# A planner that knows when each tile is written, read and loaded

## The chip, the cores and the metric

The kernel runs on one core of a Trainium2 chip. The core has five engines that take their instructions each from a list of its own, strictly in order: TensorE (PE in the profile; PEld is its weight load), VectorE (DVE), ScalarE (ACT), GpSimd (POOL) and SyncE (SP). An instruction whose operand is not there yet holds up everything behind it on its engine, and nothing on the others. Transfers between main memory and the on-chip memory are issued here by SP and by POOL, each with a queue of its own.

The metric is device time in microseconds (us) of one execution; the figure for a kernel is the median over several runs.

## The reference

The output mixes two branches, row by row, with a gate `g`. The first branch is linear attention with 32 heads of 20, the second a gated linear unit. The sequence has 2048 rows, the model width is 640, the hidden width 1536, all in fp32:

```python
phi = lambda t: where(t > 0, t + 1, exp(t)) + 1e-6
q, k, v = split(x @ wqkv)                     # 640 -> 3 x 640, 32 heads of 20
kv  = einsum("bhsd,bhse->bhde", phi(k), v)
z   = phi(k).sum(rows)
a   = (phi(q) @ kv) / (phi(q) . z + 1e-6) @ wo
b   = (sigmoid(x @ w_gate) * (x @ w_up)) @ w_down
g   = sigmoid((x * gate_w).sum(-1))
out = g * a + (1 - g) * b
```

## The kernel before

*Products.* Each fp32 operand is split into a high part, which ScalarE rounds (`split`, `act`), and a low part, which VectorE gets by subtraction. A product is then three matmuls, high by high, high by low and low by high (`mm3`, lines 216 to 218, so every matmul of the trace has one of these three lines). In the same way nearly all work of ScalarE is on line 227 and nearly all of VectorE's on line 231: the tile names tell the steps apart. Large products are cut into 2 x 2 blocks and computed with seven products of sums of blocks where eight would be the plain way. The sums are VectorE's work, the splits of the sums ScalarE's and VectorE's.

*Stages*, with their place on the trace of before: the K stage (to 142 us) makes phi(k), its sums and the products of phi(k) with x (tiles `pk`, `xn`, `gt`). Then come two passes over pairs of token groups of 512 columns, pass 1 first. Each has a q phase (`q_phase`: 142 to 191 and 414 to about 460), which makes phi(q), and in pass 1 also the attention's matrix (`kv_part`, `m_part`; tiles `wo_sb`, `woh`, `ms`), and an f phase (`f_phase`: 191 to 402, and 448 to 660), which goes over 12 chunks of the hidden width. `last_down` closes a pass; the A phase at the end (668 to 734) applies the attention's matrix and adds both branches.

*The f phase.* For each chunk f a `Block` has steps s1 to s7 (tiles `ch`, `dd`, `cc` in the accumulators; `c11`, `c12`, `c22`, `cx` in memory). Beside each odd f from 3 on runs `down_pair`, which multiplies the hidden tiles of two earlier chunks (`hf`) by the down weights (`wd`, `ds`, or `wf` in pass 0) in the products W, X0, V, X1, Y1, Y0, Z0, Z1 and adds their results to `tb`. In it `new` starts an accumulator, `go` adds a product, `out` lets ScalarE or VectorE read it into `tb`. A matmul that adds to an accumulator after an `out` has to wait until the `out` has read it. Each q or f weight comes as a `wst` tile (`load_w`) and is turned into the tiles `wg`, `wu`, `ws` by `queue_g` and `queue_s` in pass 1, stored in main memory, and loaded again in pass 0 (`load_form`). Down weights come as `dst` (`load_d`) and become `wd` and `ds`. The denominators of the attention (`queue_dens`) are a chain in pass 0: `pden` tiles are loaded, VectorE sums them into `fac`, the result goes out to memory and comes back reordered. `queue_m` splits the attention's matrix (`mr` loaded, `mt` split and stored) in pass 0 as well.

*The order.* The schedule is manual: each engine's list is the order in which the program issues. TensorE's order is written out by the phases. Everything for ScalarE and VectorE that need not follow a product at once is put in a queue of the planner `Order` (line 30): `add` takes a function with its cost on ScalarE (`a`) and VectorE (`v`), a key, and `ready`, the earliest time. While the program is written the planner keeps three modelled clocks, `pe`, `act` and `vec`. After each step `fill` takes the next item from `urgent`, `items`, `lazy`, `chain` and `spare`, in this order, if `_fits` says that it ends within a slack (0.6 and 1.2 us, or 1.6 and 2.4) of `pe`. Before a product that reads a tile `need(key)` issues what is still queued for it. Loads are believed to be there a fixed time after their issue, such as

```python
st["at", g, u] = max(order.pe, order.vec) + 9.0    # queue_dens, a pden tile
```

and a product is believed to be ready when TensorE's clock has come to it, whatever its operands. These clocks decide only the order; on the chip, semaphores make each instruction wait for its data.

Of the kernel before, what the change touches and what calls it, by code (L numbers as in the profile page):

```python
# [14 lines left out]
P = 128  # L15
# [14 lines left out]
class Order:  # L30

    def __init__(self):
        self.slack(False)
        self.pe = self.act = self.vec = 0.0
        self.items, self.lazy, self.chain, self.spare, self.soon, self.urgent = [], [], [], [], [], []
        self.kept = []
        self.busy = False
        self.parts = self.pend = None
# [5 lines left out]
    def add(self, a, v, fn, key=None, ready=None, lazy=False, first=False, chain=False, spare=False,  # L44
            kept=False):
# [27 lines left out]

    def _run(self, it):
# [12 lines left out]
    def _fits(self, it):  # L87
        a, v, fn, key, ready = it
        if ready is not None and self.pe < ready():
            return False  # L90
# [4 lines left out]
    def fill(self):  # L95
        if self.busy:
            return
        while True:
# [4 lines left out]
            for q, n in ((self.urgent, len(self.urgent)), (self.items, 1), (self.lazy, 1), (self.chain, 1), (self.spare, 1)):  # L103
# [4 lines left out]
            else:  # L108
# [5 lines left out]
                return  # L114

# [22 lines left out]
    def need(self, key, now=True):  # L138
        self.follow_up(max((i + 1 for i, f in enumerate(self.soon) if f[3] == key), default=0))
        while (it := next((it for it in self.urgent if it[3] == key), None)) is not None:  # L140
# [3 lines left out]
            if now:  # L144
                self.pe = max(self.pe, self.act, self.vec)
        for q in (self.items, self.lazy, self.chain, self.spare, self.kept):
# [3 lines left out]
            if last >= 0 or self.pend and self.pend[1] == key:  # L150
                self._flush()
                if now:
                    self.pe = max(self.pe, self.act, self.vec)
# [15 lines left out]
    def on_act(self, w, after):  # L169
        t = self._after(after)  # L170
        self.act = max(self.act, t) + a_cost(w)

    def on_vec(self, w, after, rate=1.0):
        t = self._after(after)
        self.vec = max(self.vec, t) + v_cost(w * rate)

# [9 lines left out]
def gated_mix_kernel(ctx: ExitStack, tc: tile.TileContext, xt, xn, wk, wv, wo, wst_q, wst_f, out_t):  # L186
# [6 lines left out]
    order = Order()  # L193

# [20 lines left out]
    def mm3(out, l_hi, l_lo, r_hi, r_lo, first, last):  # L215
# [3 lines left out]
        order.on_pe(3, width(out))  # L219
# [5 lines left out]
    def act(out, src, fn, after="", **kw):  # L225
        order.on_act(width(out), after)
        nc.scalar.activation(out, src, fn, **kw)  # L227

    def vec2(out, a, b, op, after=""):
        order.on_vec(width(out), after)  # L230
        nc.vector.tensor_tensor(out, a, b, op=op)  # L231

    def vec3(out, a, scalar, b, op0, op1, after=""):
        order.on_vec(width(out), after)
        nc.vector.scalar_tensor_tensor(out, a, scalar, b, op0=op0, op1=op1)

    def vec1(out, a, s0, s1=None, op0=OP.mult, op1=None, after=""):
        order.on_vec(width(out), after)
# [104 lines left out]
    class Chunk:  # L343
# [7 lines left out]
        def load(self, parts=((0, 0, KC), (1, 0, KC)), lag=0.0):  # L351
            for b, k0, k1 in parts:
                nc.sync.dma_start(self.x[b][:, k0:k1],
# [112 lines left out]
    for k in range(KC):  # L466
        nc.sync.dma_start(xst[:, 0, k], xt[0, :, k, :CW])
        if k:
            nc.sync.dma_start(wk_st[k], wk[k * P:(k + 1) * P])
        else:  # L470
            nc.sync.dma_start(wk_st[0][:, HW:], wk[:P, HW:])
        nc.sync.dma_start(xst[:, 1, k], xt[1, :, k, :CW])
# [56 lines left out]
    def queue_qw(u):  # L529

        raw = qs.tile([P, 2, D], F32, name="qraw", tag="qraw")
        nc.sync.dma_start(raw, wst_q[:, u:u + 2])
# [3 lines left out]
        def piece(i, c, src):  # L536
            n = width(src)

            def fn():
                t = qs.tile([P, 2, w], F32R, name="qp", tag="qp", bufs=2)  # L540
                split(t[:, 0, :n], t[:, 1, :n], src)
                order.then(lambda: nc.sync.dma_start(w_dram["q", u, i][:, :, c:c + n], f32(t[:, :, :n])))
# [32 lines left out]
    def load_xn(n):  # L575
        if n < 16:
            i = tok(n // 2, n % 2)
            t = m1_tile("mb", "xnst")
            nc.sync.dma_start(t, xn[i * P:(i + 1) * P])
# [24 lines left out]
    def vec_copy(out, src, after=""):  # L604
        order.on_vec(width(out), after)
# [114 lines left out]
    def z_add(r):  # L720

        nc.gpsimd.dma_start(zacc.rearrange(view2, j=2), r, accum_op=OP.add if z_started else OP.bypass)
# [115 lines left out]
    for c in range(1, 4):  # L838
# [76 lines left out]
        if c == 3:  # L915
# [23 lines left out]
            def store_w(n, i):  # L939
# [3 lines left out]
                nc.gpsimd.dma_start(w_dram[key], f32(WT[n, i]))  # L943
# [8 lines left out]
            nc.sync.dma_start(f32(WT[("q", 1, 2), 0]), w_dram["q", 2, 0])  # L952
# [17 lines left out]
        else:  # L970
            w_stage = m1_tile("ma", "w0")
            nc.sync.dma_start(w_stage, wst_q[:, KC - 1])
# [47 lines left out]
    def load_form(n, i):  # L1020
        t = (wg_tile, wu_tile, ws_tile)[i]()
        nc.sync.dma_start(f32(t), w_dram[n[::2] + (i,)])
# [7 lines left out]
    def load_w():  # L1030
        t = pw2.tile([P, 2, D], F32, name="wst", tag="wst", bufs=2)
        if not w_loads:
            t = t.rearrange("p k c -> p (k c)").rearrange("p (k c) -> p k c", c=CW)
            nc.sync.dma_start(t, xt[len(c1_x), :, :, CW:])
            c1_x.append(t)
            other[-1].at = order.pe + 4.0
            return
        n = w_loads.pop(0)
        nc.sync.dma_start(t, wst_f[n[2], :, 0:2] if n[0] == "f" else wst_q[:, 0:2])
        WST[n] = t  # L1040
        W_AT[n] = order.pe + (8.0 if n[0] == "f" else 4.0)

    def queue_q(u):
# [6 lines left out]
        order.add(a_cost(D), v_cost(D), fn, ("wg", m), lambda: DST[m][1], first=True)  # L1050

    def queue_g(n):

        order.add(a_cost(D), v_cost(D), lambda: wg_split(n, WST[n][:, 0]), ("wg", n), lambda: W_AT.get(n, 1e9),
                  first=n[2] != 1)

    def queue_s(n, first=0, last=2):

        def sums(part):
            g, u = WST[n][:, 0], WST[n][:, 1]  # L1060
            c = [slice(2 * i * P, 2 * (i + 1) * P) for i in range(2)]
            if part == 0:
                order.need(("wg", n), False)
                add(u[:, c[1]], u[:, c[0]], u[:, c[1]])
# [1315 lines left out]
```

## Time and profile before

| | |
|---|---|
| median of 3 runs | 738.40 us (738.03 to 738.62) |
| profiled execution | 739.57 us |
| its span | 737.6 us |
| TensorE busy | 729.6 us, 99% |
| VectorE busy | 563.7 us, 76% |
| ScalarE busy | 354.5 us, 48% |
| GpSimd busy | 95.2 us, 13% |
| granted TensorE clock | 1.00 |

The profile is one execution. The time of an execution is longer than the span, which goes from the first instruction to the end of the last. "Busy" counts the time in which an engine has an instruction in work; matmuls overlap each other, so that TensorE can be counted as busy while it waits a short time. In a row of the timeline stand the start, the length, the engine, the line, the operation, the tile written and the tiles read, the shape, and in brackets the idle time before it and what ended that. "x2" means two such instructions in one row.

### The profile page before, as it was taken

The numbers are of one execution on the slowest core, as the hardware profiler recorded it, in microseconds if no ns is written. First come the engines' busy times: TensorE is split into PE (matmuls) and PEld (weight loads), VectorE is DVE, ScalarE is ACT, GpSimd is POOL, SyncE is SP. The second block draws the span as 40 slices with busy tenths as digits, with TensorE's granted clock in tenths as the row PEclk, the third lists the DMA queues.
The fourth block names the chain that finished last, engine by engine and source line by source line (L and its number), as shares of the span: only waits on it lengthen the run. The fifth ranks groups of instructions, "written<-read, shape, count | busy, mean of one in ns | idle before, by whom it ended". The sixth has DMA issues, their size and how long they took to land.

```text
span 737.6 us, 10091 instructions
## 1 busy us (share of the span) xinstructions
PE 729.6 (99%) x3575; PEld 621.3 (84%) x3575; DVE 563.7 (76%) x987; ACT 354.5 (48%) x661; POOL 95.2 (13%) x161
## 2 busy tenths in 40 slices
PE   9999999999999999999999999999999999999998
PEld 8999999987777888888888888888888788888886
DVE  4988778987687889898988942447686767689993
ACT  5764638366555654535363364354423232423550
POOL 0210111123221202020200211000000032000000
PEclk9999999999999999999999999999999999999999
DMA  7573658697969766666875457967969797859212
GB/s 254 140 206 94 186 127 256 155 323 282 313 222 349 258 240 239 238 229 243 303 286 208 176 179 281 330 198 263 352 205 310 264 366 196 315 197 347 109 72 101
DMA packets 71001, 173.54 MB, mean 235 GB/s; under 512 B 11642, under 2 KB 32394, under 8 KB 67238
## 3 DMA queue, kind: packets, MB, share of 16 engines
q1 hardware_dynamic: 54582, 109.99, 45.6%
q0 software_dynamic: 16224, 62.74, 24.0%
q8 instruction: 28, 0.46, 0.3%
q14 instruction: 23, 0.19, 0.1%
q10 hardware_dynamic: 144, 0.16, 0.1%
HBM read 103.96 MB, written 63.92 MB: 228 GB/s over the span
## 4 chain that ended last, share of the span: by engine, by line
PE 89%; issue 3%; DMA 3%; ACT 2%; DVE 1%; POOL 1%; POOLq 0%; ACTq 0%
PE ch L218 9%; PE ch L216 9%; PE ch L217 9%; PE cc L216 8%; PE cc L218 7%; PE cc L217 7%; PE dd L216 7%; PE dd L217 7%; PE dd L218 7%; PE rot L216 6%; PE rot L217 6%; PE rot L218 6%; DMA wo_sb<-wo 1%; DMA wd<-ds 1%; ACT c L227 0%
## 5 line engine op out<-in xcount | busy, mean ns | idle before, releaser
L227 ACT ACTIVATE c<-ch 128x512 f32<-128x512 f32 x52 | 31.0, 597 | 95.9 <-PE ch L218 95.9
L231 DVE TENSOR_TENSOR hf<-c,hf 128x512 fp32r<-128x512 f32 x75 | 51.0, 687 | 27.9 <-ACT hf L227 27.8
L227 ACT ACTIVATE hf<-c 128x512 fp32r<-128x512 f32 x75 | 46.1, 624 | 41.0 <-DVE c L231 40.9
L231 DVE TENSOR_TENSOR c<-cc,c 128x512 f32<-128x512 f32 x40 | 27.5, 689 | 37.2 <-PE cc L218 21.2
L216 PE MATMUL ch<-xth,ws 128*128 128x512 f32 x112 | 44.2, 394 | 1.1 <-ACT c L227 0.5
L218 PE MATMUL ch<-xth,ws 128*128 128x512 f32 x112 | 43.7, 391 | 0.1
L217 PE MATMUL ch<-xtl,ws 128*128 128x512 f32 x112 | 43.6, 389 | 0.0
L231 DVE TENSOR_TENSOR tb<-rot,tb 128x512 f32<-128x512 f32 (+1 forms) x59 | 37.9, 674 | 4.7 <-PE rot L218 4.1
L231 DVE TENSOR_TENSOR tb<-dd,tb 128x512 f32<-128x512 f32 x44 | 30.1, 685 | 10.5 <-PE dd L218 10.5
L216 PE MATMUL dd<-xrh,wg 128*128 128x512 f32 x90 | 35.1, 390 | 0.0
L218 PE MATMUL dd<-xrh,wg 128*128 128x512 f32 x90 | 35.0, 389 | 0.0
L217 PE MATMUL dd<-xrl,wg 128*128 128x512 f32 x90 | 35.0, 389 | 0.0
L231 DVE TENSOR_TENSOR c<-c,c 128x512 f32<-128x512 f32 x46 | 31.6, 686 | 2.6 <-ACT c L227 2.0
L216 PE MATMUL cc<-xbh,ws 128*128 128x512 f32 x84 | 32.7, 389 | 0.0
L217 PE MATMUL cc<-xbl,ws 128*128 128x512 f32 x84 | 32.7, 389 | 0.0
L218 PE MATMUL cc<-xbh,ws 128*128 128x512 f32 x84 | 32.7, 389 | 0.0
L231 DVE TENSOR_TENSOR wst<-wst 128x256 f32<-128x256 f32 (+2 forms) x69 | 27.4, 412 | 1.4
L216 PE MATMUL rot<-pkh,xnh 128*128 128x320 f32 x90 | 28.0, 311 | 0.0
L217 PE MATMUL rot<-pkl,xnh 128*128 128x320 f32 x90 | 27.8, 309 | 0.0
L218 PE MATMUL rot<-pkh,xnl 128*128 128x320 f32 x90 | 27.8, 309 | 0.0
L227 ACT ACTIVATE c<-dd 128x512 f32<-128x512 f32 x22 | 13.0, 592 | 29.3 <-PE dd L218 26.2
L216 PEld LDWEIGHTS ch<-xth,ws 128*128 128x128 f32 x112 | 21.0, 188 | 6.8 <-ACT c L227 0.9
(648 smaller groups left out, 2318.3 us busy)
## 6 DMA issues: line engine op xcount, KB each, us to landing
wf<-ws POOLq DMA_DIRECT2D x12, 1152.0 KB, 7.6
ws<-wf SPq DMA_DIRECT2D x12, 1152.0 KB, 7.8
wst<-wst_f SPq DMA_DIRECT2D x12, 640.0 KB, 5.5
wf<-wg POOLq DMA_DIRECT2D x12, 640.0 KB, 8.0
wd<-wd POOLq DMA_DIRECT2D x12, 640.0 KB, 6.1
wg<-wf SPq DMA_DIRECT2D x12, 640.0 KB, 4.1
wf<-wd SPq DMA_DIRECT2D x10, 640.0 KB, 9.1
xnst<-xn SPq DMA_DIRECT2D x16, 320.0 KB, 4.2
```

The source lines that it names most:

```text
L216: nc.tensor.matmul(out, l_hi, r_hi, start=first, stop=False, skip_group_check=True)
L217: nc.tensor.matmul(out, l_hi, r_lo, start=False, stop=False, skip_group_check=True)
L218: nc.tensor.matmul(out, l_lo, r_hi, start=False, stop=last, skip_group_check=True)
L227: nc.scalar.activation(out, src, fn, **kw)
L231: nc.vector.tensor_tensor(out, a, b, op=op)
```

## The change

The planner gets a better picture of time, and two things are moved by hand.

1. *Times by tile.* For each tile the planner keeps when it was written and last read (`made`, `used`, `done`). A ScalarE or VectorE instruction, and now a matmul too (`mm` in place of `on_pe`), starts on its modelled clock no earlier than its operands are written and its destination is free.
2. *Queues of transfers.* `sp` and `gp` (class `Ring`) stand in for SP's and POOL's issue. They pass the transfer on unchanged, and model when it lands, with both queues sharing the bandwidth. `order.when(tile)` replaces the fixed guesses.
3. *Streams with due times.* In the f phase each step gets a place on a plan of TensorE's time (`f_steps`, `at`, `due`). Weight splits, down-weight splits and the forms of the hidden tiles go into streams, and `_stream` takes the one whose due time is nearest when it is within `EARLY` of `pe`, or when it fits.
4. `need` no longer moves the clock of TensorE.
5. `load_w` of the q phase goes from step 3 to step 6 of block A, and the splits of f = 1 from the q phase to the first steps of the f phase.
6. In `down_pair` Z1's first product and its `out` go from the start of the fourth part to the place right behind Z0's first.

The instructions and transfers are the same ones in both kernels; TensorE's order differs only by point 6, in ten down blocks.

```diff
     def _fits(self, it):
-        a, v, fn, key, ready = it
-        if ready is not None and self.pe < ready():
+        a, v, fn, key, ready = it[:5]
+        if ready is not None and max(self.pe, self.act if a else self.vec) < ready():
...
-            for q, n in ((self.urgent, len(self.urgent)), (self.items, 1), (self.lazy, 1), (self.chain, 1), (self.spare, 1)):
+            i = next((i for i, it in enumerate(self.urgent) if self._fits(it)), None)
+            if i is not None:
+                self._run(self.urgent.pop(i))
+                continue
+            name = self._stream()
+            if name is not None:
+                self._start(name)
+                continue
+            for q, n in ((self.items, 1), (self.lazy, 1), (self.chain, 1), (self.spare, 1)):
...
+    def at(self, pos):
+        if pos not in self.plan:
+            self.base = self.pe
+        self.base = self.pe - self.plan.get(pos, 0.0)
+
+    def due(self, pos):
+        return self.base + self.plan.get(pos, 1e4)
+
+    def _stream(self):
+        best = None
+        for name, q in self.streams.items():
+            if q and (q[0][4] is None or max(self.pe, self.act if q[0][0] else self.vec) >= q[0][4]()):
+                d, t = 1e9, 0.0
+                for it in q:
+                    t += max(it[0], it[1])
+                    d = min(d, it[5] - t)
+                if best is None or d < best[0]:
+                    best = (d, name)
+        if best and (best[0] <= self.pe + EARLY or self._fits(self.streams[best[1]][0])):
+            return best[1]
+        return None
...
-            if now:
-                self.pe = max(self.pe, self.act, self.vec)
+        while (name := next((n for n, q in self.streams.items() if any(it[3] == key for it in q)), None)) is not None:
+            self._start(name)
...
+    def data(self, out, aps):
+        at = max([0.0] + [self.last(self.made, self.place(ap)) for ap in aps])
+        if out is not None:
+            p = self.place(out)
+            was = self.before[p[0]]
+            at = max(at, self.last(self.used, p), self.last(self.made, p), self.end(was))
+        return at
...
+    def mm(self, out, w, first, *aps):
+        at = self.data(out if first else None, aps)
+        if not first:
+            p = self.place(out)
+            at = max(at, self.last(self.used, p), self.seeded.get(p[0], 0.0))
+        self.pe = max(self.pe, at)
+        self.pe += 0.014 + w / 2400
+        for ap in (*aps, out):
+            self.busy_till(self.place(ap)[0], [self.pe + P_LAG])
+
+    def when(self, ap):
+        return self.last(self.made, self.place(ap))
...
-    def on_act(self, w, after):
-        t = self._after(after)
+    def on_act(self, w, after, out=None, *aps):
+        t = max(self._after(after), self.data(out, aps))
         self.act = max(self.act, t) + a_cost(w)
-
-    def on_vec(self, w, after, rate=1.0):
...
+class Ring:
+
+    def __init__(self, engine, order, rings, n, issue, lag):
+        self.engine, self.order, self.rings, self.n, self.issue, self.lag = engine, order, rings, n, issue, lag
...
+    def dma_start(self, out, src, **kw):
+        o = self.order
+        start = max(self.t, o.data(out, [src]))
+        self.t = start + self.issue
+        (r1, n), (r2, _) = (self.run(ap, 0 if getattr(ap.tensor, "_space", DRAM) == DRAM else 1) for ap in (out, src))
+        r = min(r1, r2)
+        took = 1.25 * max(1, n // r) * (7 + 0.0377 * r) / 16e3
+        self.cell = self.rings.issue(self.n, start + self.lag, took)
+        o.put(out, [src], self.cell)
+        return self.engine.dma_start(out, src, **kw)
...
+    rings = Rings()
+    sp, gp = Ring(nc.sync, order, rings, 0, 0.38, 1.5), Ring(nc.gpsimd, order, rings, 1, 0.55, 2.2)
...
+    def w_due(n, s):
+        return {"stream": ("w", n), "due": order.due((*n[1:], s))} if n[0] == "f" and n[1:] + (1,) in order.plan else {}
 
     def queue_g(n):
 
-        order.add(a_cost(D), v_cost(D), lambda: wg_split(n, WST[n][:, 0]), ("wg", n), lambda: W_AT.get(n, 1e9),
-                  first=n[2] != 1)
+        order.add(a_cost(D), v_cost(D), lambda: wg_split(n, WST[n][:, 0]), ("wg", n), lambda: order.when(W_AT[n]) if n in W_AT else 1e9,
+                  first=n[2] != 1, **w_due(n, 1))
...
+                order.need(("u", n), False)
...
-            order.add(a_cost(3 * P), v_cost(3 * P), u_part, None, lambda: W_AT.get(n, 1e9))
-            order.add(0, 2 * v_cost(2 * P), lambda: sums(0))
-            order.add(0, 3 * v_cost(2 * P), lambda: sums(1))
+            order.add(a_cost(3 * P), v_cost(3 * P), u_part, ("u", n), lambda: order.when(W_AT[n]) if n in W_AT else 1e9, **w_due(n, 3))
+            order.add(0, 2 * v_cost(2 * P), lambda: sums(0), **w_due(n, 3))
+            order.add(0, 3 * v_cost(2 * P), lambda: sums(1), **w_due(n, 3))
...
-                          lambda part=part: SUM_AT.get((n, part), 1e9))
+                          lambda part=part: SUM_AT.get((n, part), 1e9), **w_due(n, 3 + part))
...
-                nc.sync.dma_start(st[g, u], p_dram[:, u, g])
-                st["at", g, u] = max(order.pe, order.vec) + 9.0
+                sp.dma_start(st[g, u], p_dram[:, u, g])
+                st["at", g, u] = lambda: order.when(st[g, u])
...
-            MO_AT[hg] = order.pe + (7.0 if hg > 1 else 9.0)
+            MO_AT[hg] = o[:w]
...
+                for j in range(2):
+                    order.need(("d", ("f", 1, 2 * p + j)), False)
...
-            order.add(0, 2 * v_cost(2 * P), lambda part=part: sums(part), lazy=p > 0)
+            order.add(0, 2 * v_cost(2 * P), lambda part=part: (sums(part), DS_AT.__setitem__(p, order.vec + V_LAG)),
+                      stream=("ds", p), due=order.due((1, 2 * p + 3, "d2")))
...
-        order.add(a_cost(D), v_cost(D), lambda: split_d(n), ("d", n), lambda: DST[n][1] if n in DST else 1e9,
-                  lazy=n[2] > 1)
+        order.add(a_cost(D), v_cost(D), lambda: split_d(n), ("d", n), lambda: order.when(DST[n][0]) if n in DST else 1e9,
+                  stream=("d", n), due=order.due((1, n[2] // 2 * 2 + 3, "d0")))
...
-        m_rows(raw, None, nc.sync, u)
-        at = max(order.pe, order.vec) + 14.0
+        m_rows(raw, None, sp, u)
...
+    def h_due(p, name):
+        seg = {"T1": 1, "B22": 1, "T2": 2, "T3": 2, "T4": 3}[name]
+        return {"stream": ("h", p), "due": order.due((order_pr[0], 2 * p + 3, 3 if name == "B22" else f"d{seg}"))}
...
-            order.add(a_cost(TG), v_cost(TG), lambda: h_form(p, name), ("h", p, name), first=True)
+            order.add(a_cost(TG), v_cost(TG), lambda: h_form(p, name), ("h", p, name), **h_due(p, name))
...
         new("Z0", "dd", "S1", "T1")
         out("Z0", 1, 1)
+        new("Z1", "cc", "S1", "T1", 1, True)
+        out("Z1", 3, 1)
         go("X0", "S3", "T3")
         out("X0", 1, 1)
         go("X1", "S3", "T3", q=1)
         out("X1", 3, 1)
         yield
-        new("Z1", "cc", "S1", "T1", 1, True)
-        out("Z1", 3, 1)
...
                     elif blk is A and s == 3:
+                        queue_g(("f", pr, 0))
+                    elif blk is A and s == 6:
                         load_w()
-                        queue_g(("f", pr, 0))
                     elif blk is A and s == 7:
                         queue_s(("f", pr, 0))
-                    elif blk is B and s == 5:
-                        queue_g(("f", pr, 1))
-                    elif blk is B and s == 6:
-                        queue_s(("f", pr, 1))
...
+    def f_steps(f):
+        down = f % 2 and f > 1
+        out = []
+        for i, e in enumerate(((f, 3), (f, 4), (f, 5), (f + 1, 1))):
+            if e[0] < FC:
+                out.append(e)
+            if down:
+                out.append((f, f"d{i}"))
+        return out + [(f, 6)] + [(f + 1, 2)] * (f + 1 < FC) + [(f, 7)]
...
+        order_pr[0] = pr
+        mm = 3 * (0.014 + TG / 2400)
+        n_mm = {1: 2, 2: 3, 3: 2, 4: 3, 5: 2, 6: 3, 7: 3, "d0": 4, "d1": 4, "d2": 6, "d3": 4}
+        at = 0.0
+        for f, s in [(0, 1), (0, 2)] + [e for f in range(FC) for e in f_steps(f)]:
+            order.plan[pr, f, s] = at
+            at += mm * n_mm[s]
+        order.plan[pr, FC + 1, "d0"] = at - EARLY
...
+            order.at((pr, f, s))
...
-                if s == 2 and 0 < f < FC - 1:
+                if s == 1 and not f:
+                    queue_g(("f", pr, 1))
+                elif s == 2 and not f:
+                    queue_s(("f", pr, 1))
+                elif s == 2 and f < FC - 1:
                     queue_g(("f", pr, f + 1))
```

271 lines of the change are left out of this document (193 added, 78 removed).

## The prediction

> **What bounds the kernel now.** I read the page first (busy shares, granted clock, chain), then busy time in 20 us windows, then the timeline of TensorE around each window that is not full, and last the rows of ScalarE, VectorE and SyncE that released each late matmul.
>
> The first fence is the page (span, engines, chain), the second the busy time by windows (length; busy of PE, PEld, DVE, ACT, POOL; granted clock; DMA share; GB/s).
>
> ```profile
> span 737.6 us, 10091 instructions
> PE 729.6 (99%) x3575; PEld 621.3 (84%) x3575; DVE 563.7 (76%) x987; ACT 354.5 (48%) x661; POOL 95.2 (13%) x161
> PE 89%; issue 3%; DMA 3%; ACT 2%; DVE 1%; POOL 1%; POOLq 0%; ACTq 0%
> ```
>
> ```profile
> 180.00:200.00 20.00, 18.06 (x79) 14.28 (x79) 13.98 (x24) 14.08 (x25) 7.10 (x12) 1.00 0.81 274
> 220.00:240.00 20.00, 19.48 (x85) 15.44 (x84) 15.01 (x32) 12.12 (x25) 3.24 (x7) 1.00 0.93 352
> 560.00:580.00 20.00, 19.63 (x85) 15.59 (x85) 13.79 (x23) 5.43 (x10) 0.00 (x0) 1.00 0.80 270
> ```
>
> TensorE is busy 99% of the span at a granted clock of 1.00, and the chain is 89% matmuls. The change keeps all matmuls, so it can only win back time in which TensorE waits for an operand, and can only lose by making new waits. VectorE (76%) and ScalarE (48%) have room on average. The windows lose 1.94, 0.52 and 0.37 us: short single stalls, not a slow stretch. Busy time hides the smallest, since the rows of matmuls overlap; I therefore count from start to start. A row of 128x512 follows its predecessor by 0.227 us (227.65 to 227.88 below, and the same over the rows that follow without a wait); what is above that is stall.
>
> ```profile
> 179.61 0.40 PE L218 MATMUL ch<-xth,ws 128*128 128x512 f32 x1
> 180.89 0.39 PE L216 MATMUL dd<-woh,kvh 100*100 100x320 f32 x1 [0.89 <-ACT ms L227]
> ...
> 190.28 0.39 PE L218 MATMUL dd<-xrh,wg 128*128 128x512 f32 x1
> 191.12 0.50 PE L216 MATMUL ch<-xth,ws 128*128 128x512 f32 x1 [0.45 <-ACT c L227]
> ...
> 218.91 0.39 PE L218 MATMUL cc<-xbh,wu 128*128 128x512 f32 x1
> 219.59 0.50 PE L216 MATMUL ch<-xth,ws 128*128 128x512 f32 x1 [0.29 <-ACT cx L227]
> ...
> 227.65 0.39 PE L218 MATMUL cc<-xbh,ws 128*128 128x512 f32 x1
> 227.88 0.39 PE L216 MATMUL cc<-xbh,ws 128*128 128x512 f32 x1
> ...
> 228.33 0.39 PE L218 MATMUL cc<-xbh,ws 128*128 128x512 f32 x1
> 229.11 0.50 PE L216 MATMUL ch<-xth,ws 128*128 128x512 f32 x1 [0.39 <-ACT ws L227]
> ...
> 230.31 0.40 PE L216 MATMUL ch<-xth,ws 128*128 128x512 f32 x1
> ...
> 278.49 0.39 PE L218 MATMUL dd<-hf,ds 128*128 128x512 f32 x1
> 278.94 0.47 PE L216 MATMUL rot<-hf,ds 128*128 128x512 f32 x1
> ...
> 381.13 0.39 PE L218 MATMUL rot<-hf,wd 128*128 128x512 f32 x1
> 381.70 0.50 PE L216 MATMUL dd<-hf,wd 128*128 128x512 f32 x1 [0.18 <-ACT dd L227]
> ...
> 576.68 0.39 PE L218 MATMUL rot<-hf,wf 128*128 128x512 f32 x1
> 577.44 0.50 PE L216 MATMUL cc<-hf,wf 128*128 128x512 f32 x1 [0.37 <-DVE tb L231]
> ...
> 645.61 0.39 PE L218 MATMUL dd<-hf,wf 128*128 128x512 f32 x1
> 645.97 0.50 PE L216 MATMUL rot<-hf,wf 128*128 128x512 f32 x1
> 646.31 0.40 PE L217 MATMUL rot<-hf,wf 128*128 128x512 f32 x1
> ```
>
> Stalls, in order: 1.05 (1.28-0.227), 0.61, 0.45, then 228.33 to 230.31 with four starts in 1.98 us, 1.07 above four times 0.227; the pair gap 0.22 at 278.49; 0.34 at 381; 0.53 at 576. At 645 the start is late by 0.13 and the next by another 0.11: 0.24 together. That same second row slips by about 0.11 behind 190, 218, 381 and 576 too. The gap of 278 and 645 stands in eight of the ten down blocks (first and last shown): 8 x 0.23 = 1.8.
>
> **The change, part by part.** No instruction or DMA is added or removed. TensorE's order changes only in ten Z1 groups of three matmuls; on ScalarE, VectorE, SyncE and GpSimd's queue the same instructions are permuted. The bookkeeping costs nothing on the chip: it runs while the program is written.
>
> ```profile
> 176.93 0.74 ACT L227 ACTIVATE woh<-wo_sb 100x640 fp32r<-100x640 f32 x1 [2.14 <-DMA wo_sb<-wo]
> ...
> 187.23 0.83 DVE L231 TENSOR_TENSOR wg<-wst,wg 128x640 fp32r<-128x640 f32 x1 [0.90 <-ACT wg L227]
> ...
> 228.32 1.26 ACT L227 ACTIVATE ws<-wst 128x640 fp32r<-128x640 f32 x2 [0.95 <-DVE wst L231]
> ...
> 278.12 1.28 DVE L231 TENSOR_TENSOR tb<-rot,tb 128x512 f32<-128x512 f32 x2
> ```
>
> *Z1 one place forward.* At 278.49 X0's third product must wait until VectorE has read X0 (the tb rows, 1.28 us for two). Three matmuls of Z1, 3 x 0.227 = 0.68 us, now stand between, more than the 0.23 missing. X0's output then has 0.45 to spare, and Z1's own second product gets two products more of distance from its output, which is the wait at 576.68. Gain 1.8, and 0.53+0.11 at 576. Its cover is the 0.68: where VectorE is later than that, the gap returns in part.
>
> *Weight loads and splits at the end of the q phase* (`load_w` from A's step 3 to step 6, gate and up splits of f=1 into the f phase). In the row at 176.93 ScalarE waits 2.14 us for wo_sb, whose load had been put behind the 640 KB wst load on SyncE; now both last wo_sb loads stand ahead of it. But f=0's two ws splits (1.26 us for such a pair at 228.32) move ahead of the last ms evictions. If the wait goes, 2.14-1.26 = 0.9 us is left over, and that is nearly the stall: I take the whole 1.05 as gained; if it stays, the splits come on top, and the other end is a loss of 1.26. At 190 the wg low half (187.23) and both ScalarE splits go behind the late eviction: gain 0.61+0.11.
>
> *Streams with due times in the f phase.* At 218 and 228 down-weight sums (dst), ds and ws splits stood ahead of the operand needed next. They have due times now and stand up to 16 us later; ds is not read before the next down block. Gain 0.45+0.11 and 1.07. At 381 an xah split stood ahead of the dd seed and is behind it now: 0.34+0.10. Gains: 1.05+0.72+0.56+1.07+1.8+0.44+0.64 = 6.3.
>
> ```profile
> 28.27 0.48 DVE L606 COPY gt<-dd 128x320 f32<-128x320 f32 x1
> 28.68 0.95 DVE L231 TENSOR_TENSOR xbl<-xst,xbh 128x768 fp32r<-128x768 f32 x1
> 29.54 0.48 DVE L606 COPY gt<-rot 128x320 f32<-128x320 f32 x1
> 29.94 0.41 DVE L231 TENSOR_TENSOR b12l<-xst,b12h 128x256 fp32r<-128x256 f32 x1
> 30.27 0.88 DVE L231 TENSOR_TENSOR xst<-xst 128x256 f32<-128x256 f32 x2
> ...
> 30.44 0.31 PE L216 MATMUL rot<-pkh,xnh 128*128 128x320 f32 x1
> ```
>
> *The K stage, first loss.* VectorE is full here. xbl now stands ahead of gt from dd, and b12l and one xst sum ahead of gt from rot. Starting from 28.27: xbl 0.86, gt 0.40, b12l 0.33, xst 0.45, then gt 0.48 gives an end at 30.79, where the matmul that reuses the bank starts at 30.44: 0.4 us late. Around 62 xal, xrl, xbl and an xst sum pass another gt in the same way, by the same durations some 0.3 late. The lower bound is 0 (VectorE catches up before TensorE is through), the upper twice that, 1.4. I take 0.7, what the durations give.
>
> *Chains that wait for DMAs in pass 0.* The guessed landing times (9 us for pden, 14 for mr) are replaced by a queue model: 1.5 us lag, 0.5 completion, and for pden's 256 KB 0.84 transfer, 2.8 in all. The trace:
>
> ```profile
> L1210 SPq DMA_DIRECT2D pden<-p_dram x20: 319/320/544, 488.6 to 588.8; - x20
> ...
> DMA to landing us min/median/max: 2.8/5.9/10.8
> ...
> DMA to landing us min/median/max: 1.9/4.4/8.0
> ...
> 573.93 0.55 DVE L242 TENSOR_SCALAR fac<-pden,zcol,zeps 128x512 f32<-128x512 f32 x1 [1.45 <-DMA pden<-p_dram]
> ```
>
> The first two rows are pden, the third mr, the last a wait of VectorE for pden. So 2.8 is the best case. From 494 to 518 four fac steps now stand ahead of an eviction of cc and four more ahead of the tb adds that free rot; three mt splits on ScalarE stand ahead of c and dd evictions. Both engines serve in order, so a late load holds these up and through them TensorE. Of the 1.45 us that VectorE waited at 573.93, 0.53 reached TensorE at 576: a share of 0.37. At the medians pden lands 5.9-2.8 = 3.1 after the model's time, mr about 2.1 (4.4 against 2.0 and 0.3 of transfer); one such wait each, at 0.37, is 1.9. At the shortest landings it is 0, at the longest (8.0 and 5.7 late) 5.1. I take 0.9, half of the median case: the model lets transfers queue behind each other, so part of the 3.1 is in the plan. Behind the waiting steps stand, on SyncE, the f=6 and f=7 weight loads; those are needed more than 20 us later.
>
> The Trainium skill (DMA: Bandwidth & Descriptors, Anatomy of one DMA) gives 2.0 us plus bytes over 436 GB/s for one transfer, an estimated 2.6 for pden; by it this term is 0. The trace's 2.8 agrees as a minimum, its median of 5.9 doesn't.
>
> *The rest.* Everything else is moved where I find at least 0.2 us before the matmul that reads it (mostly 0.5 to 5): the A phase, the last down step, ws splits of pass 1. With this many permutations one new stall of the median size seen before (0.5) is likely: 0.5.
>
> Sum: -6.3+0.7+0.9+0.5 = -4.2 us. The profiled execution took 739.57 (2.0 around the span), so 735.4 and a span of 733.4. The median of the runs is 738.40, 1.17 below the profiled one; with the same difference 734.2. A measurement can tell about 0.2% (1.5 us).
>
> **Rivals.** *In-order waits for DMAs (slower).* Place: ScalarE and VectorE from 488 to 600, 20 pden and 5 mt steps. For it: a pden median 3.1 us above the model. If ten pairs of pden steps each wait that long and 0.37 of it reaches TensorE, the price is 11.5; it decides from the 5.6 us that are gained otherwise (6.3-0.7), that is, from five pairs. Against it: the queueing in the plan, and few other loads on SyncE there. With seven of the ten (8.0): 738.4-5.6+8.0 = 740.8. The Trainium skill (SBUF — State Buffer, SBUF: two separate sides) adds that transfers issued by GpSimd can be held up by VectorE's two-port copies; the plan's fixed 2.2 us for that queue knows nothing of it, and no run here shows it yet.
>
> *wo_sb still late.* For it: 1.26 us of ws splits in front; against it: two loads ahead of wst. The stall at 180 stays and grows: 1.05 not gained and 1.26 lost, 734.2+2.3 = 736.5.
>
> *Z1 moved for nothing.* VectorE, given other work in the 0.68 us, reads X0 later too: 1.8+0.64 not gained, 736.6.
>
> *Gains and new stalls cancel.* K stage 1.4, waits 3 (between 1.9 and 5.1), three more stalls of 0.5: -6.3+5.9, 738.0.
>
> **How the numbers follow.** Forecast 734.2, 0.56; wo_sb 0.08; Z1 0.08; cancel 0.12; DMA waits 0.16. Faster by over 0.2%: forecast, wo_sb, most of Z1: 0.71; within: 0.12 with what is left of those, 0.13; slower 0.16. Range: low where every loss is nothing, 738.4-6.3 = 732.1; the likeliest case's own range is 732.1 to 736.6; to leave out no more than 2 in 10 it takes in the cancelling case and the near part of the slow one: 739.4.
>
> **What would show it.** Right: no row above 0.3 us idle on TensorE at 180, 190, 218, 228; X0's third product directly behind Z1's first at 0.227; the 180:200 window at 19 or more. Wrong: idle ahead of mt on ScalarE or fac on VectorE in 490 to 600 with TensorE rows waiting behind; stalls at 29 to 31 and 62 over 0.5; ScalarE still waiting for wo_sb near 177.

## The result, and the profile after

The changed kernel takes 734.81 us (median of 6 runs, 733.88 to 736.75), the kernel before 738.51 (6 runs, 738.03 to 738.74). The ratio is 0.9952, with a 95% interval of 0.9939 to 0.9965: 3.7 us are won. The profiled execution took 734.86 with a span of 733.0, against 739.57 and 737.6.

The page of the changed kernel (span, engines, chain), and its busy time by windows, with the columns of the prediction:

```profile
span 733.0 us, 10098 instructions
PE 726.5 (99%) x3575; PEld 622.3 (85%) x3575; DVE 561.6 (77%) x987; ACT 355.4 (48%) x661; POOL 94.5 (13%) x161
PE 93%; DMA 2%; issue 2%; DVE 1%; ACT 1%; POOL 1%; SPq 0%; POOLq 0%; DVEq 0%; ACTq 0%
```

```profile
180.00:200.00 20.00, 19.41 (x86) 15.23 (x85) 13.89 (x23) 12.75 (x23) 5.99 (x11) 1.00 0.80 275
220.00:240.00 20.00, 20.00 (x90) 16.46 (x89) 16.02 (x34) 14.33 (x27) 3.79 (x7) 1.00 0.76 270
560.00:580.00 20.00, 20.00 (x90) 16.56 (x89) 17.78 (x29) 4.34 (x8) 0.00 (x0) 1.00 0.63 224
```

The same engines have the same work, and matmuls now make up 93% of the chain instead of 89%. The windows of 220 and 560 are full; that of 180 still lacks 0.6 us. The timeline of TensorE shows what is gone and what is new:

```profile
62.81 0.31 PE L406 MATMUL rot<-pkh,xnl 128*128 128x320 f32 x1
63.23 0.41 PE L404 MATMUL rot<-pkh,xnh 128*128 128x320 f32 x1
...
180.23 0.40 PE L406 MATMUL ch<-xth,ws 128*128 128x512 f32 x1
180.84 0.39 PE L404 MATMUL dd<-woh,kvh 100*100 100x320 f32 x1 [0.21 <-ACT ms L417]
...
195.40 0.39 PE L406 MATMUL ch<-xah,wg 128*128 128x512 f32 x1
196.16 0.50 PE L404 MATMUL ch<-xth,wu 128*128 128x512 f32 x1 [0.38 <-ACT cx L417]
...
276.38 0.39 PE L406 MATMUL cc<-hf,ds 128*128 128x512 f32 x1
276.61 0.39 PE L404 MATMUL rot<-hf,ds 128*128 128x512 f32 x1
...
496.61 0.39 PE L406 MATMUL dd<-hf,wf 128*128 128x512 f32 x1
498.41 0.50 PE L404 MATMUL rot<-hf,wf 128*128 128x512 f32 x1 [1.41 <-DVE tb L421]
```

X0's third product follows Z1's first at 0.23 (276.38 to 276.61); the gap in front of it is gone in every down block. The stalls at 190, 218, 228, 381 and 576 have no row left that is more than 0.11 late. What remains or is new: about 0.1 in each of four rows at 29.6 to 31, 0.27 at 62.8 (a row of 320 columns follows the last at 0.145), 0.38 at 180, 0.53 at 196, and 1.57 at 496.6, in front of X0's fourth product. What made them late stands on VectorE and ScalarE:

```profile
490.03 1.21 DVE L432 TENSOR_SCALAR fac<-pden,zcol,zeps 128x512 f32<-128x512 f32 x2 [2.18 <-DMA pden<-p_dram]
491.44 1.42 DVE L425 SCALAR_TENSOR_TENSOR fac<-pden,zcol,fac 128x512 f32<-128x512 f32 x2 [0.20 <-DMA pden<-p_dram]
492.77 0.82 DVE L421 TENSOR_TENSOR mt<-mr,mt 128x640 fp32r<-128x640 f32 x1
493.51 0.68 DVE L421 TENSOR_TENSOR c<-cc,c 128x512 f32<-128x512 f32 x1
494.11 2.28 DVE L425 SCALAR_TENSOR_TENSOR fac<-pden,zcol,fac 128x512 f32<-128x512 f32 x3
497.00 0.75 DVE L425 SCALAR_TENSOR_TENSOR fac<-pden,zcol,fac 128x512 f32<-128x512 f32 x1 [0.61 <-DMA pden<-p_dram]
497.67 1.28 DVE L421 TENSOR_TENSOR tb<-rot,tb 128x512 f32<-128x512 f32 x2
```

```profile
179.22 1.24 ACT L417 ACTIVATE ws<-wst 128x640 fp32r<-128x640 f32 x2
180.36 0.74 ACT L417 ACTIVATE ms<-dd 100x320 f32<-100x320 f32 x2
...
189.88 1.28 ACT L417 ACT_TABLE_LOAD   x1
...
194.89 0.74 ACT L417 ACTIVATE ws<-wst 128x640 fp32r<-128x640 f32 x1 [2.19 <-DVE wst L421]
195.53 0.58 ACT L417 ACTIVATE cx<-ch 128x512 f32<-128x512 f32 x1
...
499.80 0.74 ACT L417 ACTIVATE mt<-mr 128x640 fp32r<-128x640 f32 x1 [5.56 <-DMA mr<-m_dram]
```

At 490 to 498 VectorE waits three times for pden (3.0 us together), and the adds that free rot stand behind; ScalarE waits 5.6 us for mr at the same time. At 180 the ws splits stand ahead of the ms evictions, at 196 one stands ahead of the cx eviction.

If each matmul is set beside the same matmul of before, the shift between the two traces can be read place by place (minus is earlier):

| place | term of the prediction | shift measured |
|---|---|---|
| K stage, 29 to 31 and 62 | +0.7 | +0.85 |
| 94 | none | -0.3 |
| 180 to 183 | -1.05 | -1.8 |
| 190 | -0.72 | -0.66 |
| 196 | none ("one new stall", +0.5) | +0.65 |
| 218 | -0.56 | -0.52 |
| 228 to 230 | -1.07 | -1.09 |
| gaps in eight down blocks | -1.8 | -2.4 |
| 381 | -0.44 | -0.43 |
| 497 | +0.9 | +1.65 |
| 576 | -0.64 | -0.64 |
| last matmul | -4.2 | -4.65 |

The two profiled executions are 4.7 us apart and the medians 3.7: the profiled execution of the kernel before stands 1.1 us above the median of its runs, that of the changed kernel at its median.

### The profile page after: what moved, and what is told of

The parts are those of the page before. It is cut to its first block, busy times and chain, and to the rows that moved or that the text cites. A ratio compares the mean times of both kernels' runs of the same rounds, so it can differ in the third digit from the quotient of the medians.

```text
span 733.0 us, 10098 instructions
## 1 busy us (share of the span) xinstructions
PE 726.5 (99%) x3575; PEld 622.3 (85%) x3575; DVE 561.6 (77%) x987; ACT 355.4 (48%) x661; POOL 94.5 (13%) x161
## 4 chain that ended last, share of the span: by engine, by line
PE 93%; DMA 2%; issue 2%; DVE 1%; ACT 1%; POOL 1%; SPq 0%; POOLq 0%; DVEq 0%; ACTq 0%
PE ch L404 10%; PE ch L406 10%; PE ch L405 10%; PE cc L404 8%; PE cc L406 8%; PE cc L405 8%; PE dd L404 7%; PE dd L405 7%; PE dd L406 7%; PE rot L404 6%; PE rot L405 6%; PE rot L406 6%; DMA pden<-p_dram 1%; DMA p_dram<-qe 1%; PE rot L1521 1%
## 5 line engine op out<-in xcount | busy, mean ns | idle before, releaser
L417 ACT ACTIVATE dd<-ch 128x512 f32<-128x512 f32 x22 | 12.8, 582 | 33.6 <-PE ch L406 33.6
```

## The experiments

The theory: each term has the cause that the prediction names, Z1's place, the moves at the end of the q phase, the due times, and, as losses, the K stage and the waits for pden. Rivals stand with each run. "Excess" below is a start-to-start distance above the usual one, as in the prediction. Beside these runs the kernel before took 738.9 (e1 to e4), 739.22 (e5 to e8) and 739.72 us (e9 to e12), so the ratios compare better than the times; that of the changed kernel is 0.9952.

**e1_z1_alone.** The kernel before, with only this:

```diff
         out("Z0", 1, 1)
+        new("Z1", "cc", "S1", "T1", 1, True)
+        out("Z1", 3, 1)
         go("X0", "S3", "T3")
...
         yield
-        new("Z1", "cc", "S1", "T1", 1, True)
-        out("Z1", 3, 1)
```

> Kernel before with Z1's first product and output one place forward, nothing else. If the eight gaps in front of X0's third product are closed by the three matmuls of Z1 alone, they go (8 x 0.23 = 1.8 us) and so does the late start of Z1's second product at 576 (0.64): 736.1 to 736.7. The rival, that VectorE is given other work in the 0.68 us and reads X0 later too: gaps stay, 738.5.

Measured: 737.4 us, ratio to the kernel before 0.9981 (0.9969 to 0.9993). All eight gaps go, and the stalls at 381 and 576 too (0.21 stands at 574, in front of another product of a down block). But the old planner, whose order shifts with TensorE's, now lets a ws split come late in four places of pass 1 (about 0.37 each, 1.5 together). The first in the trace:

```profile
266.70 0.39 PE L217 MATMUL ch<-xtl,ws 128*128 128x512 f32 x1
267.19 0.50 PE L218 MATMUL ch<-xth,ws 128*128 128x512 f32 x1
```

So Z1's place closes the gaps by itself, as expected, and the 1.4 us won by the ratio are a good half of the 2.4 expected, since the old order gave much back. The stall at 180 is 0.43 here and not 1.05, though the order up to there is that of the kernel before: its size differs between executions.

**e2_z1_back.** The changed kernel with the opposite edit.

> Changed kernel with Z1 where it stood before. If the gain of the down blocks belongs to Z1's place, the gaps of 0.22 to 0.24 return in eight blocks: 1.8 to 2.4 us above the changed kernel, about 736.6 to 737.2. If the new planner closes them by itself (it knows when the accumulator is read), the time stays at 734.8.

Measured: 736.49, ratio 0.9967 (0.9954 to 0.9981). All eight gaps are back (seven of 0.22 to 0.24, one of 0.47), 2.1 us in all; the new planner does not close them. The time rose by less, since in this order the stall at 497 is only 0.11. VectorE's first two waits for pden are those of the changed kernel (2.23 and 0.22 us), but Z1's three matmuls (0.68 us) again stand in front of X0's fourth product, and one fac step (0.74) stands behind the add that frees rot. So Z1's move also takes 0.68 us of cover from that product. The waits at 381 and 576 stay away, so that this part of the gain belongs to the planner as well as to Z1 (e1 removed both alone).

**e3_pden_guess.** The changed kernel with the old belief about pden:

```diff
-                st["at", g, u] = lambda: order.when(st[g, u])
+                at = max(order.pe, order.vec) + 9.0
+                st["at", g, u] = lambda: at
```

> Changed kernel in which a pden tile counts as landed 9 us after its issue, as before, and not when the queue model says. If the 1.57 us stall at 496.6 comes from VectorE waiting for pden loads (2.18, 0.20 and 0.61 us) ahead of the tb reads, it goes: 1.5 to 1.7 us below the changed kernel, about 733.1. If the mt split on ScalarE, which waits 5.6 us for mr at 494, is the cause, the stall stays and the time with it (734.8).

Measured: 734.82, ratio 0.9944 (0.9927 to 0.9961). The stall at 497 is gone, so the waits for pden cause it. But hardly any time is won: one of 1.23 stands at 566, behind a pden wait of VectorE that the fixed guess, blind to SyncE's queue, had not seen:

```profile
566.01 0.55 DVE L432 TENSOR_SCALAR fac<-pden,zcol,zeps 128x512 f32<-128x512 f32 x1 [2.62 <-DMA pden<-p_dram]
```

**e4_mr_guess.** The changed kernel with the old belief about mr:

```diff
+        at = max(order.pe, order.vec) + 14.0
...
-        order.add(a_cost(D), v_cost(D), fn, "m", lambda: order.when(raw), spare=True)
+        order.add(a_cost(D), v_cost(D), fn, "m", lambda: at, spare=True)
```

> Changed kernel in which an mr tile counts as landed 14 us after its issue, as before. If ScalarE's 5.6 us wait for mr at 494 (and the second of the kind, 8.4 us together) is what makes TensorE late at 496.6, 1.5 to 1.7 us are won (733.1). If the pden waits on VectorE are the cause, ScalarE's wait goes and the stall stays within 0.3 us: 734.5 to 735.1.

Measured: 734.19, ratio 0.9941 (0.992 to 0.9963). ScalarE no longer waits for mr, and the stall stays, at 1.06 instead of 1.57:

```profile
497.09 0.39 PE L406 MATMUL dd<-hf,wf 128*128 128x512 f32 x1
498.38 0.50 PE L404 MATMUL rot<-hf,wf 128*128 128x512 f32 x1 [0.90 <-DVE tb L421]
```

It moved by 0.5, more than the 0.3 expected: VectorE's mt step (0.82 us at 492.77 in the changed kernel) no longer stands ahead of the add that frees rot, while its waits for pden there grew from 3.0 to 3.4 us. The 5.6 us wait of ScalarE cost nothing by itself: in the changed kernel no late row of TensorE between 494 and 510 was released by ScalarE.

**e5_k_clock.** The changed kernel; TensorE's modelled clock ignores late operands until the K stage is over:

```diff
-        self.pe = max(self.pe, at)
+        if self.live:
+            self.pe = max(self.pe, at)
...
+    order.live = True
```

> Changed kernel in which TensorE's modelled clock ignores late operands until the end of the K stage, as before, and follows them afterwards. If the K stage's new stalls come from that clock (it runs later, so more splits seem to fit ahead of the gt copies), the late starts at 29.6, 30.9 and 62.8 go and 0.6 to 0.8 us are won: 734.1. The rival, that the later due copies come from the queue model or from the clocks of ScalarE and VectorE: order and stalls stay, 734.8. What follows the K stage (0.38 at 180, 0.54 at 196, 1.57 at 497) stays within 0.2 us.

Measured: 734.46, ratio 0.9932 (0.9911 to 0.9953). The late starts at 29.6, 30.9 and 62.8 are gone, and the gt copies stand ahead of xbl again. Their cause is that clock: it now counts waits, so the planner believes TensorE later than it is and lets more work in front. The stall at 497 grew to 1.92, against the expectation, and took back 0.35 of the 0.8 gained in the K stage.

**e6_pden_later.** The changed kernel; a pden tile counts as landed at the later of the guess and the model:

```diff
-                st["at", g, u] = lambda: order.when(st[g, u])
+                at = max(order.pe, order.vec) + 9.0
+                st["at", g, u] = lambda: max(at, order.when(st[g, u]))
```

> Changed kernel in which a pden tile counts as landed at the later of two times: 9 us after its issue, and when the queue model says. If one of the two bounds alone lets VectorE run into a wait (the model near 490, the fixed guess near 566), both stalls are gone: no gap above 0.3 us on TensorE after 200, and 1.5 to 1.7 us below the changed kernel, 733.2. If waits for other transfers take their place, a gap of 0.5 to 1.5 us stands elsewhere between 480 and 600 and the time stays at 734 to 735.

Measured: 732.8, ratio 0.9909 (0.9889 to 0.993). VectorE never waits for pden, and no excess above 0.12 is left on TensorE after 200. This is the price of the step: the queue model alone cost 1.7 us, and beside a bound from before it costs nothing.

**e7_q_back.** The changed kernel with the weight load and the splits of f = 1 back in the q phase:

```diff
                     elif blk is A and s == 3:
+                        load_w()
                         queue_g(("f", pr, 0))
-                    elif blk is A and s == 6:
-                        load_w()
...
+                    elif blk is B and s == 5:
+                        queue_g(("f", pr, 1))
+                    elif blk is B and s == 6:
+                        queue_s(("f", pr, 1))
...
-                if s == 1 and not f:
-                    queue_g(("f", pr, 1))
-                elif s == 2 and not f:
-                    queue_s(("f", pr, 1))
-                elif s == 2 and f < FC - 1:
+                if s == 2 and 0 < f < FC - 1:
```

> Changed kernel with the weight load back at step 3 of block A and the splits of f = 1 back in the q phase. If the gains at 180 and 190 come from these two moves, the stalls of before return (1.05 by the wait for wo_sb, 0.7 by the splits ahead of the eviction) and those of after go (0.38 at 180, 0.64 at 196): 0.5 to 0.9 us above the changed kernel, 735.5. If the planner's new clocks alone had removed them, there is no stall at 190 and the time falls to about 734.1.

Measured: 738.43, ratio 0.999 (0.9971 to 1.0008): nearly everything is lost again, 2.8 us by the ratios, about four times what was expected. The stall at 180 is 0.38, as with the moves, and ScalarE doesn't wait for the last wo_sb. The stall at 190 is not 0.7 but 2.97, and the matmuls behind it are slow:

```profile
188.86 0.39 PE L406 MATMUL dd<-xrh,wg 128*128 128x512 f32 x1
192.06 0.79 PE L404 MATMUL ch<-xth,ws 128*128 128x512 f32 x1 [2.81 <-ACT c L417]
192.65 0.63 PE L405 MATMUL ch<-xtl,ws 128*128 128x512 f32 x1
193.08 0.63 PE L406 MATMUL ch<-xth,ws 128*128 128x512 f32 x1
193.51 0.63 PE L404 MATMUL ch<-xth,ws 128*128 128x512 f32 x1
```

```profile
192.00:195.00 3.00, 2.94 (x7) 2.36 (x8) 2.63 (x4) 1.92 (x3) 0.54 (x1) 0.50 0.93 326
```

**e8_down_lazy.** The changed kernel with the down weights' sums and splits (`queue_ds`, `queue_df`, `queue_d`) in the lazy queue, as before, in each of the three like this (the ready time of `queue_df` goes as well, which the kernel before does not have):

```diff
-                      stream=("ds", p), due=order.due((1, 2 * p + 3, "d2")))
+                      lazy=p > 0)
```

> Changed kernel with the down weights' splits and sums in the lazy queue, as before, and all else in streams. If the due times of the down weights remove the stalls that stood at 218 and 228 (0.56 and 1.07), these return in whole or part: 0.6 to 1.6 us above the changed kernel, 735.4 to 736.4. If the better clocks remove them, the time stays within 0.3 us of 734.8.

Measured: 737.22, ratio 0.9973 (0.996 to 0.9987). The stalls at 218 and 228 do not return: the new clocks and the streams that are left keep the down weights out of the way there even without due times of their own. Instead ds itself is late where it is needed, with 1.8 us of excess in four steps:

```profile
237.46 0.39 PE L406 MATMUL ch<-xth,ws 128*128 128x512 f32 x1
239.05 0.50 PE L404 MATMUL rot<-hf,ds 128*128 128x512 f32 x1 [1.20 <-ACT ds L417]
```

So the due times are worth about what the prediction gave them, but by making ds come in time.

**e9_table.** The changed kernel; the planner counts the load of the function table:

```diff
+        if fn in (AF.Exp, AF.Sigmoid) and fn != table[0]:
+            table[0] = fn
+            order.act += 1.28
```

> Changed kernel in which the planner's ScalarE clock also counts the 1.28 us load of the function table in front of the first sigmoid and at each later switch. If the stall at 196 (0.53 and 0.11) comes from that load, which makes the wu split, the wst sums and with them the ws split late that stands ahead of the cx eviction, the split now stands behind it and the stall goes: 0.6 us below the changed kernel, 734.2, with the stalls at 180 and 497 unchanged within 0.3. If the load has nothing to do with it, 196 stays at 0.6.

Measured: 734.25, ratio 0.9941 (0.9916 to 0.9966). The stall at 196 is gone, that at 180 is the same 0.38. The one at 497 grew to 2.04, which hides most of the gain.

**e10_base.** The changed kernel; the plan of the first f phase begins at the q phase's end:

```diff
         order_pr[0] = pr
+        if pr:
+            order.base = order.pe + 48.0
```

> Changed kernel in which the plan of the first f phase begins 48 us after the q phase's start (its length on the trace) and not at zero. In the changed kernel the splits of f = 0 are queued against a plan that begins at zero, so that their due times lie in the past and they are taken at once, ahead of the ms evictions. If that is the stall at 180, it goes (0.38), and the splits of f = 1 may fall behind the cx eviction too (0.64 at 196): 0.4 to 1.0 us below the changed kernel, 733.8 to 734.4. The rival, that the ms evictions are late by themselves: 0.38 stays.

Measured: 733.3, ratio 0.9922 (0.9895 to 0.9949). The stalls at 180 and at 196 are both gone, as expected; the ms evictions come first. That at 497 happens to be 0.74.

**e12_q_back_base.** e7 with the plan's start of e10.

> The weight load and the splits of f = 1 back in the q phase, with the plan starting at 48 us. If the 2.97 us stall that this showed at 188.9 came from due times in the past (the splits of f = 1 were taken at once, ahead of a late eviction), it falls to 0.7 or less: 2 us or more below that run, 735 to 736.2. If the place of the splits itself is the cause, it stays above 2 us. With the wst load ahead of the last wo_sb load ScalarE waits 1.5 to 2.1 us for wo_sb as in the kernel before if the order of the two loads decides that wait; without a wait here the order of the loads does not decide it.

Measured: 736.41, ratio 0.9958 (0.9943 to 0.9973). The stall at 188.6 is 2.21, above the 2 us set for the rival: a better due time takes only 0.8 from it, and the slow matmuls behind it are gone as well (1.4); together that is about the 2.0 us by which the time fell. What remains belongs to the two moves: e10, which differs from this run by them alone, has no stall here.

```profile
188.61 0.39 PE L406 MATMUL dd<-xrh,wg 128*128 128x512 f32 x1
191.05 0.50 PE L404 MATMUL ch<-xth,ws 128*128 128x512 f32 x1 [2.05 <-ACT c L417]
```

```profile
175.21 0.73 ACT L417 ACTIVATE woh<-wo_sb 100x640 fp32r<-100x640 f32 x1
```

The row of woh has no wait, although wst is issued ahead of the last wo_sb load, as before. The order of these two loads does not decide that wait.

In the kernel before the same place of the splits costs 0.61 and not 2.21. ScalarE's eviction that TensorE waits for, first here, then in the kernel before:

```profile
190.42 0.58 ACT L417 ACTIVATE c<-ch 128x512 f32<-128x512 f32 x1
```

```profile
190.49 0.58 ACT L227 ACTIVATE c<-ch 128x512 f32<-128x512 f32 x1
```

It comes at the same time in both. But TensorE, which in the kernel before has lost time in the stall at 180, comes to this place at 190.28 there and at 188.61 here. What is won at 180 is waited out again at 190 as long as the splits stand there, so the two gains are not independent.

**e11_all.** The edits of e5, e6, e9 and e10 together.

> The four repairs together: TensorE's clock as before in the K stage, pden at the later of two times, the table load counted, the plan's start. If the stalls are independent, those at 30, 63, 180, 196 and 497 all go (0.33, 0.37, 0.38, 0.64, 1.68, 3.4 in all): 731.4 and a ratio to the kernel before of 0.990 to 0.991. If one repair moves work into another's way, one or two stalls of 0.3 to 1.5 us stand in new places: 732 to 733.

Measured: 730.88, ratio to the kernel before 0.9887 (0.9871 to 0.9903), 0.5 below the expectation. No excess above 0.12 us is left behind the first 10 us (six rows at 145 to 169 that start 0.32 us after the last, 0.09 more than usual, stand in all kernels):

```profile
span 729.1 us, 10102 instructions
PE 99%; DVE 0%; issue 0%
```

```profile
180.00:200.00 20.00, 20.00 (x91) 16.56 (x90) 14.06 (x23) 12.81 (x23) 5.88 (x11) 1.00 0.78 263
480.00:500.00 20.00, 20.00 (x90) 16.49 (x89) 12.14 (x19) 12.44 (x23) 1.27 (x2) 1.00 0.86 276
```

The chain is 99% matmuls, against 89% before the change. This version is 8.8 us faster than the kernel before on its chip (739.72), and faster than the changed kernel.

## Why the prediction was right

The time (734.2 against 734.81), the range and the sign held, and so did most terms of the sum in place and kind. That the sum came so near is in part luck: the gains at 180 and in the down blocks were counted 1.4 us too low, the losses about 1.1 too low, and these errors cancel. Nor did the step from the trace to the median hold, which took the profiled execution to stand 1.17 us above it: that of the changed kernel stands at its median. Point by point:

- *Z1 one place forward* was right in place and cause (e1, e2). Its term was a little low: the gaps gave 2.4 where eight times 0.23 were counted, since the late second rows in pass 1 (0.08 each) and some small later waits go too. That the wait at 576 is Z1's was only half right: each of the two parts of the change removes it. What the step left out is that the move takes 0.68 us of cover from X0's fourth product, where the stall at 497 stands (e2).
- *Weight loads and splits at the end of the q phase.* Here the step failed in its reason. "Both last wo_sb loads stand ahead of" wst was taken as the cause of the gain at 180. e7 and e12 have the old order of these loads and no wait. One thing that differs is GpSimd's store of wg, which goes out at 168.0 in the kernel before and at about 170.7 in the others, so that it runs beside the wo_sb load for a shorter time (in e1 it goes out at 169.4, and the wait is 1.50). Another is that SyncE issues the wst load before it at 158.1 there and at about 156.6 in e7 and e12. No run isolates either, and the cause of the 2.14 us wait stays open. The ws splits ahead of ms, which the step named as the risk, did leave 0.38, and the reason is a plan that begins at zero (e10). The term came out at 1.8 in place of 1.05, because two further waits in the same group of matmuls, at 181.85 and 182.86, were not counted. At 190 the step was right in its cause: with the splits back in the q phase the stall is 2.2 (e12). Its price of 0.72 holds only for a TensorE that is late from 180; taken as one of two independent gains it was too small.
- *Streams with due times.* The sizes were right (0.52 and 1.09 for 0.56 and 1.07), the cause was not wholly: without the due times of the down weights the two stalls stay away, and a later one of 1.8 us comes in (e8). The wait at 381, put down to this step as well, goes by Z1's move alone too (e1). No run takes the due times from the weight splits or the hidden tiles, and none tests point 4 of the change by itself.
- *The K stage* was right in place and size (+0.85 for +0.7). The durations of the rows, laid end to end in the new order, were enough. The cause, TensorE's modelled clock, was not in the prediction (e5).
- *Chains that wait for DMAs in pass 0*: right in kind and place, mis-sized: +1.65 for the 0.9 taken, near the 1.9 worked out for the median landings. The guess that the model's queueing foresees half of the lateness was too kind. The share that reaches TensorE was 1.57 of 3.0, 0.52 and not 0.37, and a share was the wrong form for it. The 0.37 came from one wait. In the same trace of before VectorE waits three times as long at another place, and no row of TensorE is late there:

```profile
599.66 0.75 DVE L235 SCALAR_TENSOR_TENSOR fac<-pden,zcol,fac 128x512 f32<-128x512 f32 x1 [4.47 <-DMA pden<-p_dram]
```

In seven kernels the same eight fac steps and the mt step stand ahead of the add that frees rot. There VectorE's waits for pden come to 2.28, 2.60, 2.99, 3.20, 3.26, 3.64 and 3.68 us (e10, e12, the changed kernel, e8, e7, e5, e9), and the stalls to 0.74, 1.05, 1.57, 1.48, 1.70, 1.92 and 2.04: always 1.4 to 1.7 less. So what reaches TensorE is the wait less the time that VectorE has to spare at that place, and a few tenths in a landing decide its size. The mr half of the step was wrong: ScalarE's wait of 5.6 us cost nothing (e4).
- *The rest*: one new stall of 0.5 was taken, one of 0.65 came, at 196. e9 gives its cause, a table load of 1.28 us on ScalarE that the planner does not count; the later start of the plan removes it too (e10).
- Of the rivals, the in-order wait for transfers came true once and not seven times. The slower outcome needed five pairs of pden steps; two groups of four steps ahead of one add decided here.

## What to carry to other kernels

Where a planner decides the order, read the new order against the old trace: lay the measured durations end to end up to the matmul that waits, and add up stalls by start-to-start distances, all rows of a group and not its first alone. A wait costs what is left of it behind the slack of its place, so read that slack for each place instead of a share, and ask of each stall that goes whether the next place is then reached too early. A model of transfers that fits the unqueued case should not replace a guess with a margin; the later of the two was worth 1.7 us. When a planner's clocks get better, look for what they do not count: here a plan's start and a table load left the stalls at 180 and 196.

## What the runs showed that was not expected

- A wait of 2.81 us was followed by seven matmuls that took 0.3 to 0.6 us from start to start where 0.227 is usual, 1.4 us more in all, and the granted clock of 192 to 195 us was 0.50 (e7). Waits of 2.05 us (e12) and 1.88 us were followed by a single row that is 0.11 late. The Trainium skill (TensorE: Matmul & The Clock Gate, What's actually happening) puts the fall to half clock behind an idle window of about 3.4 us; here, in one trace, 2.81 us were enough. So this stall of 2.97 us cost half as much again.
- The rows of TensorE in the first 7 us differ between executions whose first instructions are the same ones: the start up to 20 us had about 1.8 to 2.8 us of excess in the traces, with matmuls of 322 columns 0.27 us apart, where 0.148 is usual, up to 6.6 us in some. That is a microsecond of spread before the kernel's order matters, as large as most terms of this prediction.
